# Attention and two MLPs on one core: other homes and another order for the first five pairs of heads

## The chip, the cores and the metric

The kernel runs on one core of one Trainium2 chip. The metric is the device time of one execution in microseconds. Three executions of the kernel before took 939.34, 941.24 and 942.3 us; the median is 941.24 us. The profile comes from one more execution, which took 943.38 us.

## The reference

Causal attention with a bias per position, for 4 batches of 8 heads, 576 positions and 64 elements a head, and then two MLPs over the 2304 tokens. The core of it:

```python
scores = scale * np.matmul(q, k.transpose(0, 1, 3, 2))
s_pos = np.maximum(s, 0.0)
cum = np.cumsum(s_pos, axis=-1)
bias = -(cum[:, :, :, None] - cum[:, :, None, :])
scores = np.where(causal, -1000000000.0, scores + np.minimum(bias, 0.0))
scores = scores - np.max(scores, axis=-1, keepdims=True)
attn = np.exp(scores)
attn = attn / (np.sum(attn, axis=-1, keepdims=True) + 1e-09)
attn_out = np.matmul(attn, v)
# x = attn_out as (2304, 512)
h = x @ w_in;   r = np.maximum(h, 0.0);  x = (r * r) @ w_out      # first MLP
h = x @ w2_in;  out = np.maximum(0.01 * h, h) @ w2_out            # second MLP
```

All inputs and outputs are float32. d_model is 512, d_ff is 2048.

## The kernel before, in words

The 32 heads are worked off as 16 pairs. A pair lies on the 128 partitions as two heads of 64. Its 576 query rows are cut into four kinds of work: kind 0 (query tiles 0 and 1), kind 2, kind 3 (query tiles 2 and 3) and kind 4 (the last 64 rows of both heads in one tile). `STEPS` gives seven slots a pair: two each (one per head, `e`) for kinds 0, 2 and 3, and one for kind 4. The loop over `y` in `attention` goes through the 112 slots of the 16 pairs.

For one kind the work goes through four engines. TensorE makes the scores (`scores`, L458 and L470) into a PSUM tile `S` or `h`. VectorE adds the mask, stores the sum in an SBUF tile `t` and takes the row maximum (`maxima`, L486). ScalarE takes the exponential in place and sums the row (`exponentials`, L510). TensorE transposes `t` in 64-row pieces into two PSUM banks with the tag `tr` (`flip`, L525), and ScalarE (kinds 0 and 2, L548) or VectorE (kinds 3 and 4, L546) copies them into `pT0`, `pT1` and `pX`. `values` (L567) multiplies `v` with these: region 0 is the first 256 query rows, region 1 the other 320. `gather` (L577, ScalarE) copies the product to `xo`; `inverse`, `spread` and `scale` (L583, L584, L602, L608, L612) divide it by the row sums; `store` sends it to DRAM.

What sets the order:

- The tile `t` has four buffers (`TB`), taken in turn by every slot. The tag `tr` has four banks, taken in turn by `flip`, `values` and `spread`: 12 in a pair, so that each use finds the same bank in each pair. A use waits until the reader of the bank's last content is done.
- `S` is one tile of two banks, `h` are two banks. In the first five pairs kinds 0 and 3 write `S`, kinds 2 and 4 write `h`. So the scores of kind 3 wait until both reductions of kind 0 are done, and the scores of kind 0 of the next pair wait until both of kind 3 are.
- `Y` holds a pair's turned q and k, in four quarters: `ql`, `kh`, `qh`, `kl`. In pairs 0 to 4 (`x < PLAIN`) the scores are plain float32 products, and only `kh` and `qh` are written (`turn`, L428); the quarters 0 and 3 lie unused. From pair 5 on all four are used.
- TensorE's order within a slot is written by hand (`in_order`). On VectorE and ScalarE a scheduler sets the order when the program is built.

Between these run two other streams: the weights of the first MLP are loaded and cut into two parts (`load_w`, L114, L118, L120, L122, L123, L170, L173), two chunks in five slots from slot 11 on; and from slot 36 on, after pair 4, `fill` puts products of the first MLP (L655) between the steps of attention. Pairs 0 to 4 are `ALONE`: they have no such filling on TensorE. The products of the first MLP's block 0 need the output of pairs 0 to 3.

Within pairs 0 to 4 `values` of region 0 comes in slot 6 and of region 1 in slot 10 (counted from the pair's first, so in the next pair's slot 3), and `gather` one slot later. In the slot in which region 1 of pair x is multiplied, kind 0 of pair x + 1 is transposed, behind it.

Of the kernel before, what the change touches and what calls it, by code (L numbers as in the profile page):

```python
# [8 lines left out]
F32 = mybir.dt.float32  # L9
# [14 lines left out]
def attention_then_two_mlps(  # L24
# [28 lines left out]
    P = 128  # L53
# [20 lines left out]
    AHEAD = 20  # L74
    PLAIN = 5
    ALONE = 5
    KINDS = (0, 2, 3, 4)
    STEPS = ((0, 0), (0, 1), (2, 0), (2, 1), (3, 0), (3, 1), (4, 0))

# [395 lines left out]
    def maxima(at, x, kind, e):  # L475

        p = pairs[x]
        t = at.tile([P, S], F32, tag="t", name="t", bufs=TB)
        m = at.tile([P, 16], F32, tag="m", name="m", bufs=TB + 1)

        def reduce(sc, msk, a, z, first, m):
            return nc.vector.tensor_tensor_reduce(t[:, a:z], sc, msk, -QK_SCALE, first, ALU.add, ALU.min, m).ins  # L486

        sc = p.sc[kind][e]
        if kind == 0:
            tiles = ((0, P, 0), (P, 3 * P, 1))  # L490
            for a, z, c in tiles:
                done = reduce(sc[:, a:z], mask[:, S - z + a:], a, z, 3.0e38, m[:, c:c + 1])
        elif kind == 4:
            tiles = ((0, S, 0),)
            reduce(sc[:, :S // 2], mask[:, :S // 2], 0, S // 2, 3.0e38, m[:, 1:2])
            done = reduce(p.sc[kind][1][:, :S // 2], mask4, S // 2, S, m[:, 1:2], m[:, 0:1])
        else:
            tiles = ((0, (kind + 1) * P, 0),)
            done = reduce(sc[:, :(kind + 1) * P], mask[:, S - (kind + 1) * P:], 0, (kind + 1) * P, 3.0e38, m[:, 0:1])
        if kind == 0 and e == 0:  # L500
            p.sums = at.tile([P, 16], F32, tag="sums", name="sums", bufs=4)
        T = {0: 0, 2: 2, 3: 3, 4: 4}[kind]
        p.t = t
        return t, m, tiles, p.sums, 2 * T + e, done

    def exponentials(t, m, tiles, sums, c0):
# [4 lines left out]
                                        accum_out=sums[:, s0:s0 + 1])  # L511
        return done.ins

    def flip(at, x, kind, ts):

        p = pairs[x]
        banks = [bank("tr") for _ in range(2)]
        w = 3 if kind == 0 else kind + 1
        n = 0
        for t in ts:  # L520
            for c in range(w):
                a = min(c * P, S - P)
                for r in range(2):
                    hs = slice(64 * r, 64 * r + 64)
                    nc.tensor.transpose(banks[r][:, 64 * n:64 * n + 64], t[hs, a:a + P], ident[hs, hs])  # L525
                n += 1
        if kind == 0:
            p.pT[0] = at.tile([P, 2, 3, P], F32, tag="pT0", name="pT0")
        if kind == 2:
# [20 lines left out]
    def values(x, region):  # L550
# [5 lines left out]
        for c in range(2 if region == 0 else 5):  # L556
# [4 lines left out]
                mm.append((c, a, [p.pT[1][:, e, c, a:] for e in range(2)]))  # L561
            else:
                mm.append((c, NR1 - 64, [p.pX[:, 1 - e] for e in range(2)]))
        start = len(nc.cur_bb.bb.instructions)
        for y, (c, a, rhs) in enumerate(mm):
            for e in range(2):
# [96 lines left out]
    def attention(at, mg, mx):  # L663
# [131 lines left out]
        for y in range(end + 14):  # L795
# [6 lines left out]
                behind = [args[-1], exponentials(*args[:-1])]  # L802
            fill(y, 0)
            tiled = len(nc.cur_bb.bb.instructions)
            for px in (x - 1, x):
                if not 0 <= px < len(pairs):
                    continue
                k0 = y - n * px
                for region in range(2):
                    if k0 == values_at(px, region):  # L810
                        pairs[px].po[region] = values(px, region)
            for z in (y - LAG, y - 1):
                zx, zs = divmod(z, n)
                kind, e = STEPS[zs]
                if 0 <= z < end and (e or kind == 4) and (z == y - 1) == (kind == 3 and zx >= ALONE):
                    flip(at, zx, kind, [live.pop(i) for i in range(z - e, z + 1)])
            if y + 1 < end and STEPS[(y + 1) % n][1] == 0:
                last = len(KINDS) * x + KINDS.index(STEPS[st][0])
                while asked <= last + (2 if last + 2 < AHEAD else 1):
# [4 lines left out]
            for px in (x - 1, x):  # L824
# [1 line left out]
                    continue  # L826
                k0 = y - n * px
                for region in range(2):
                    if k0 == values_at(px, region) + 1:
                        gather(at, px, region, pairs[px].po[region])  # L830
                portions = ((9, 0, 2), (13, 2, 5)) if px < ALONE else ((13, 0, 5),)
                for when, a, b in portions:
# [323 lines left out]
```

## Time and profile before

| | |
|---|---|
| median of 3 runs | 941.24 us |
| lowest, highest | 939.34, 942.3 us |
| the profiled execution | 943.38 us |
| its span, first to last instruction | 941.6 us |
| TensorE busy | 902.7 us (96%) |
| VectorE busy | 708.2 us (75%) |
| ScalarE busy | 578.6 us (61%) |
| GpSimd busy | 181.8 us (19%) |

The span lies 1.78 us under the execution's own time. The first 93 us of the span are the pairs without filling (0 to 4) and the step into pair 5; attention with filling ends at about 335 us. In the tables of stretches below, each engine has its busy microseconds and, in brackets, its number of instructions; PEclk is TensorE's granted clock, where 1.00 is 2.4 GHz and 0.50 is 1.2 GHz.

### The profile page before, as it was taken

How to read it: one execution, taken by the hardware profiler on the slowest of the kernel's cores; microseconds unless marked ns; L12 is line 12 of the kernel's file. 1: busy time of each engine (PE TensorE's matmuls, PEld its weight loads, DVE VectorE, ACT ScalarE, POOL GpSimd, SP SyncE). 2: the span in 40 equal slices, each digit the busy share in tenths (PEclk: the TensorE clock that was granted, in tenths of full speed). 3: DMA queues.
4: the chain of work that ended last, by engine and by line, in shares of the span. 5: the costliest groups of instructions: out<-in, count | busy, mean ns of one | idle time of the engine just before them, and what ended most of it. 6: DMA issues, size and time to landing. Idle time of an engine off the chain costs nothing.

```text
span 941.6 us, 16406 instructions
## 1 busy us (share of the span) xinstructions
PE 902.7 (96%) x5902; PEld 809.2 (86%) x5902; DVE 708.2 (75%) x1286; ACT 578.6 (61%) x1076; POOL 181.8 (19%) x290
## 2 busy tenths in 40 slices
PE   5877999999999999999999999999999999999997
PEld 3545777777777778989999999999999999999997
DVE  6789774877784348489797898788478788786974
ACT  5687877877796444366565555586677764344442
POOL 4357652333350001000213101001111000000000
PEclk9988999999999999999999999999999999999999
DMA  8865847896954177857749434767758585727303
GB/s 158 183 166 146 209 129 192 234 239 212 240 175 159 58 235 278 294 200 231 241 133 339 163 107 149 242 219 281 275 189 313 183 268 137 184 51 204 97 12 56
DMA packets 229569, 178.48 MB, mean 190 GB/s; under 512 B 139600, under 2 KB 206352, under 8 KB 229488
## 3 DMA queue, kind: packets, MB, share of 16 engines
q1 hardware_dynamic: 192568, 105.13, 41.5%
q10 hardware_dynamic: 27048, 38.16, 11.1%
q0 software_dynamic: 9872, 34.15, 10.5%
q8 instruction: 46, 0.75, 0.3%
q14 instruction: 35, 0.29, 0.1%
HBM read 111.25 MB, written 66.13 MB: 188 GB/s over the span
## 4 chain that ended last, share of the span: by engine, by line
PE 56%; issue 10%; DVE 6%; DMA 6%; ACT 2%; POOL 1%; ACTq 0%; SPq 0%; POOLq 0%; DVEq 0%
PE q L858 34%; PE h L655 16%; DVE op L965 3%; PE tr L567 2%; PE S L470 2%; PE tr L525 2%; DMA gp<-gscr 1%; DMA gp<-zscr 1%; DMA gp<-qscr 1%; PE S L458 1%; DVE gp L959 1%; DMA zscr<-post 1%; DMA xscr<-xo 1%; DVE wt L122 1%; POOL zscr L1027 1%
## 5 line engine op out<-in xcount | busy, mean ns | idle before, releaser
L858 PE MATMUL q<-op,w 128*128 128x384 f32 x3024 | 527.9, 335 | 6.5 <-DVE op L965 4.3
L858 PEld LDWEIGHTS q<-op,w 128*128 128x128 f32 x3024 | 523.6, 188 | 10.5 <-DVE op L965 6.6
L964 ACT ACTIVATE op<-gp 128x768 fp32r<-128x768 f32 x189 | 158.0, 845 | 152.1 <-PE q L858 125.4
L655 PE MATMUL h<-xs,w 128*128 128x512 f32 (+1 forms) x960 | 213.1, 376 | 2.3 <-DVE xs L616 1.7
L965 DVE TENSOR_TENSOR op<-gp,op 128x768 fp32r<-128x768 f32 x189 | 177.7, 952 | 40.6 <-ACT op L964 39.3
L655 PEld LDWEIGHTS h<-xs,w 128*128 128x128 f32 x960 | 164.5, 190 | 40.0 <-issue 6.0
L510 ACT ACTIVATE t<-t,m 128x128 f32<-128x128 f32 (+2 forms) x144 | 83.2, 579 | 48.6 <-DVE m L486 44.1
L486 DVE CUSTOM_DVE_ANT_0 t<-S,mask 128x128 f32<-128x128 f32 (+2 forms) x129 | 56.3, 476 | 49.2 <-PE S L470 24.0
L638 ACT ACTIVATE gs<-h 128x512 f32<-128x512 f32 (+1 forms) x80 | 43.7, 548 | 46.3 <-PE h L655 45.8
L186 POOL DMA_DIRECT2D wscr<-wt x48 | 26.7, 555 | 233.5 <-DVE wt L123 231.8
L931 DVE TENSOR_TENSOR post<-q,post 128x768 f32<-128x768 f32 (+1 forms) x55 | 51.6, 939 | 15.6 <-PE q L858 15.2
L567 PE MATMUL tr<-pT,v 128*64 128x320 f32 (+3 forms) x384 | 50.1, 405 | 5.0 <-DVE pT L546 5.0
L470 PE MATMUL S<-Y 64*128 64x128 f32 (+3 forms) x324 | 41.5, 373 | 12.8 <-DVE Y L428 7.5
L123 DVE SCALAR_TENSOR_TENSOR wt<-wst,wt 128x512 uint32<-128x512 uint32 x64 | 50.4, 787 | 3.9 <-POOL wt L122 3.2
L911 ACT ACTIVATE post<-q 128x768 f32<-128x768 f32 (+1 forms) x56 | 43.8, 782 | 12.5 <-PE q L858 12.4
L114 ACT ACTIVATE wt<-wst 128x512 f32<-128x512 f32 x64 | 42.2, 660 | 12.9 <-DMA wst<-in_moe_w_in_dram 7.9
L567 PEld LDWEIGHTS tr<-pT,v 128*64 128x64 f32 x384 | 25.9, 143 | 27.8 <-issue 7.8
L525 PEld LDWEIGHTS tr<-ident,t 64*128 64x128 f32 x800 | 31.3, 138 | 21.3 <-issue 8.0
L118 DVE TENSOR_SCALAR wt<-wt 128x512 uint32<-128x512 uint32 x64 | 32.7, 511 | 20.0 <-ACT wt L114 19.6
L891 ACT ACTIVATE post<-post 128x768 f32<-128x768 f32 x36 | 30.4, 844 | 26.0 <-DVE post L931 25.8
L525 PE MATMUL tr<-ident,t 64*128 64x64 f32 x800 | 39.6, 230 | 5.4 <-ACT xo L577 4.9
L199 DVE TENSOR_TENSOR w<-wq,w 128x512 fp32r<-128x512 f32 x49 | 33.3, 687 | 14.7 <-ACT w L198 14.7
(115 smaller groups left out, 918.6 us busy)
## 6 DMA issues: line engine op xcount, KB each, us to landing
gscr<-gs ACTq DMA_DIRECT2D x36, 512.0 KB
gp<-gscr SPq DMA_DIRECT2D x48, 384.0 KB
qscr<-post ACTq DMA_DIRECT2D x48, 384.0 KB
gp<-qscr SPq DMA_DIRECT2D x48, 384.0 KB
wscr<-wt POOLq DMA_DIRECT2D x48, 256.0 KB, 4.4
wst<-in_moe_w_in_dram SPq DMA_DIRECT2D x19, 512.0 KB
wst<-in_moe_w_out_dram SPq DMA_DIRECT2D x16, 512.0 KB
wst<-in_moe_w_out_dram POOLq DMA_DIRECT2D x16, 512.0 KB, 5.0
```

Of the source, the lines that this page charges most:

```text
L123: nc.vector.scalar_tensor_tensor(t, hw, 0xC0000000, t, ALU.bitwise_and, ALU.bitwise_or)
L470: nc.tensor.matmul(p.sc[kind][e][:, a:z], qs[hs, T * P:(T + 1) * P], ks[hs, :z - a], start=(n == 0 and y == 0), stop=(n == len(tiles) - 1 ...
L486: return nc.vector.tensor_tensor_reduce(t[:, a:z], sc, msk, -QK_SCALE, first, ALU.add, ALU.min, m).ins
L510: done = nc.scalar.activation(t[:, a:z], t[:, a:z], AF.Exp, bias=m[:, c:c + 1], scale=-1.0, accum_out=sums[:, s0:s0 + 1])
L525: nc.tensor.transpose(banks[r][:, 64 * n:64 * n + 64], t[hs, a:a + P], ident[hs, hs])
L567: p.anchor = nc.tensor.matmul(po[64 * e:64 * e + 64, a:n], p.vr[:, c, e], rhs[e], start=(y == 0), stop=(y == len(mm) - 1), skip_group_chec ...
L655: nc.tensor.matmul(h[:, :w], win[fc][:, a, c * P:(c + 1) * P], xs[j, c][:, z, :w], start=(c == 0 and y == 0), stop=(c == KC - 1 and y == 2))
L858: i = nc.tensor.matmul(*args, skip_group_check=True, **kw).ins
L911: done = nc.scalar.activation(t[:, xs], acc, AF.Copy)
L931: done = nc.vector.tensor_tensor(t[:, xs], acc, t[:, xs], ALU.add)
L964: a = nc.scalar.activation(t[:, 0], src, AF.Copy)
L965: c = nc.vector.tensor_tensor(t[:, 1], src, f32(t[:, 0]), ALU.subtract)
```

## The change

Four edits, all for pairs 0 to 4. First, kind 3's masked scores and exponentials go into the unused quarters 0 and 3 of `Y` instead of two buffers of `t`, so that only five slots in seven take a buffer of `t`. Second, in the slot in which region 1 is multiplied with v, the transposes of the next pair's kind 0 now stand ahead of that product. Third, `gather` of region 0 is written one slot earlier in the source. Fourth, TensorE multiplies the identity with itself into banks whose content nobody reads: 512 columns ahead of kind 4's transposes in pairs 0 to 4, 256 columns ahead of region 1's product in pairs 0 to 3, and three times 128 columns behind kind 4's transposes in pair 4.

```diff
+    WARM = 5
@@ maxima
-        t = at.tile([P, S], F32, tag="t", name="t", bufs=TB)
+        if kind == 3 and x < PLAIN:
+            t = f32(p.Y[:, 3 * e])
+        else:
+            t = at.tile([P, S], F32, tag="t", name="t", bufs=TB)
@@
+    def idle(to):
+
+        n = to.shape[1] // P
+        nc.tensor.matmul(to, ident, ident.unsqueeze(1).to_broadcast([P, n, P]), start=True, stop=True)
+
@@ flip
+        if kind == 4 and x < WARM:
+            idle(banks[0])
...
+        if kind == 4 and x == WARM - 1:
+            for _ in range(3):
+                idle(banks[1][:, 3 * P:])
@@ values
+        if region and x < WARM - 1:
+            idle(po[:, :2 * P])
@@ attention
-            for px in (x - 1, x):
...
-                        pairs[px].po[region] = values(px, region)
-            for z in (y - LAG, y - 1):
...
+            for early in (True, False):
+                for px in (x - 1, x):
+                    if early or not 0 <= px < len(pairs):
+                        continue
...
+                            pairs[px].po[region] = values(px, region)
+                for z in (y - LAG, y - 1):
...
+                    if early != (kind == 0 and zx < ALONE):
+                        continue
...
-                    if k0 == values_at(px, region) + 1:
+                    if k0 == values_at(px, region) + (region or px >= ALONE):
                         gather(at, px, region, pairs[px].po[region])
```

TensorE, the stretch in pair 4's time in which region 1 of pair 3 is multiplied. `tr` are the banks of transposes and products with v, `ident` the identity, `ex` the row sums' inverses, `S` the scores of kind 3. Before, from the transposes of kinds 3 and 4 (one run of 26) to those of kind 0:

```order
L525 MATMUL tr<-ident,t 128x64 x26
L470 MATMUL S<-Y 128x512 x2
L470 MATMUL S<-ag_88 128x512 x2
L602 MATMUL tr<-ident,ex 128x128 x2
L567 MATMUL tr<-pT_889,v 64x320 x6
L567 MATMUL tr<-pT_889,v 64x192 x2
L567 MATMUL tr<-pX,v 64x64 x2
L525 MATMUL tr<-ident,t 128x64 x12
```

The same stretch of the changed kernel:

```order
L536 MATMUL tr<-ident,Y 128x64 x16
L521 MATMUL tr<-ident 128x512
L536 MATMUL tr<-ident,t 128x64 x10
L471 MATMUL S<-Y 128x512 x2
L471 MATMUL S<-ag_88 128x512 x2
L618 MATMUL tr<-ident,ex 128x128 x2
L536 MATMUL tr<-ident,t 128x64 x12
L521 MATMUL tr<-ident 128x256
L583 MATMUL tr<-pT_887,v 64x320 x6
L583 MATMUL tr<-pT_887,v 64x192 x2
L583 MATMUL tr<-pX,v 64x64 x2
```

The twelve transposes of kind 0 moved ahead of the product with v, kind 3's sixteen read `Y`, and the two products of the identity stand ahead of kind 4's transposes and ahead of the product with v.

VectorE, the start of pair 2. `S` and `h` are scores, `m` the row maxima, `kr` and `qr` the raw keys and queries of pair 3, `sums` the row sums, `wt` a chunk of weights. Before, from the first transpose of pair 3's keys to the first copy of pair 1's kind 4:

```order
L428 STREAM_TRANSPOSE Y<-kr 128x576
L123 SCALAR_TENSOR_TENSOR wt<-wst,wt 128x512
L486 ISA t,m<-S,mask 128x128
L486 ISA m 128x1
L486 ISA t,m<-S,mask 128x256
L486 ISA m 128x1
L428 STREAM_TRANSPOSE Y<-qr 128x576
L546 COPY pT_456<-tr 128x8x64 x2
L486 ISA t,m<-h,mask 128x384
L486 ISA m 128x1
L546 COPY pT_456<-tr 128x4x64
```

In the changed kernel, where all four reductions of kind 0 stand directly ahead of this piece and the copies of kind 4 behind it:

```order
L119 TENSOR_SCALAR wt<-wt 128x512
L624 TENSOR_TENSOR xo<-xo,tr 128x256
L628 TENSOR_TENSOR xo<-xo,tr 64x64 x2
L490 ISA t,m<-h,mask 128x384
L490 ISA m 128x1
L599 TENSOR_SCALAR sums<-sums 128x4
L124 SCALAR_TENSOR_TENSOR wt<-wst,wt 128x512
L600 RECIPROCAL sums<-sums 128x4
L119 TENSOR_SCALAR wt<-wt 128x512
L560 COPY pT_454<-tr 128x8x64 x2
L429 STREAM_TRANSPOSE Y<-kr 128x576
L429 STREAM_TRANSPOSE Y<-qr 128x576
```

The two transposes of keys and queries moved from between the reductions of kind 0 to between the copies of kinds 3 and 4; the sums of kind 0, which need its exponentials, moved from behind the copies to ahead of them; and pair 0's last scaling of `xo` and two steps on weights came in.

ScalarE, the same place: from the end of pair 1 to the exponentials of pair 2's kind 0 (128 and 256 columns, twice). `pT` are copies of transposes, `wt` and `wst` steps on weights. Before:

```order
L548 ACTIVATE pT_456<-tr 128x2x3x64 x2
L510 ACTIVATE t,sums<-t,m 128x576
L114 ACTIVATE wt<-wst 128x512
L120 ACTIVATE wst<-wst 128x512
L577 ACTIVATE xo<-tr 128x256
L510 ACTIVATE t,sums<-t,m 128x128
L510 ACTIVATE t,sums<-t,m 128x256
L510 ACTIVATE t,sums<-t,m 128x128
```

And in the changed kernel:

```order
L514 ACTIVATE t,sums<-t,m 128x576
L562 ACTIVATE pT_454<-tr 128x2x3x64 x2
L115 ACTIVATE wt<-wst 128x512
L121 ACTIVATE wst<-wst 128x512
L514 ACTIVATE t,sums<-t,m 128x128
L514 ACTIVATE t,sums<-t,m 128x256
L514 ACTIVATE t,sums<-t,m 128x128
L593 ACTIVATE xo<-tr 128x256
L514 ACTIVATE t,sums<-t,m 128x256
```

The exponentials of kind 4 moved ahead of kind 2's copies, and the gather of region 0 into `xo` (L577, now L593) moved from ahead of kind 0's exponentials to behind three of the four.

## Rows read from the trace of the kernel before

**Rows 1.** Busy time by stretch: start:end, length, engines, clock.
```profile
93.30:335.00 241.70, 241.36 (x1918) 184.22 (x1918) 159.00 (x436) 178.78 (x426) 86.36 (x128) 1.00 0.66 185
```

**Rows 2.** The same view, from a pair's first reduction to the product of region 1.
```profile
19.57:25.64 6.07, 2.22 (x22) 1.07 (x19) 5.20 (x21) 2.92 (x11) 0.00 (x0) 0.99 0.70 142
35.00:41.01 6.01, 3.16 (x41) 1.83 (x37) 5.78 (x20) 4.65 (x15) 3.22 (x5) 1.00 0.93 167
47.94:56.38 8.44, 5.42 (x45) 2.65 (x41) 8.05 (x24) 6.72 (x22) 5.55 (x8) 0.79 0.49 134
64.92:71.86 6.94, 3.95 (x44) 2.28 (x44) 6.90 (x22) 6.94 (x20) 6.10 (x7) 1.00 1.08 237
```

**Rows 3.** The same view, the product of region 1 with v in three pairs.
```profile
25.64:29.47 3.83, 3.83 (x20) 1.94 (x21) 0.94 (x5) 0.71 (x2) 1.31 (x5) 0.56 0.87 275
41.01:43.21 2.20, 2.20 (x20) 1.34 (x21) 1.37 (x7) 0.71 (x2) 1.28 (x2) 1.00 0.83 152
56.38:60.20 3.82, 3.82 (x20) 1.91 (x20) 1.37 (x7) 1.60 (x4) 2.57 (x2) 0.57 0.47 137
```

**Rows 4.** The same view, pair 4 and the step into the filled part.
```profile
64.92:82.05 17.13, 12.40 (x138) 8.21 (x138) 16.21 (x45) 14.36 (x40) 13.62 (x17) 1.00 0.92 213
82.05:93.30 11.25, 7.82 (x36) 5.41 (x36) 10.44 (x27) 8.97 (x24) 9.03 (x9) 0.70 0.33 103
```

**Rows 5.** VectorE's and TensorE's waits, 10 to 95 us: total, times, longest.
```profile
DVE t L486 <- PE tr L525: 7.3, 4, 3.3
...
PE tr L525 <- ACT xo L577: 4.9, 4, 2.0
```

**Rows 6.** VectorE in order of time: start, duration, line, tiles, wait before.
```profile
10.32 0.29 DVE L486 CUSTOM_DVE_ANT_0 t<-S,mask 128x128 f32<-128x128 f32 x1 [2.90 <-PE S L470]
...
11.44 0.77 DVE L428 STREAM_TRANSPOSE Y<-kr 128x576 f32<-128x576 f32 x1
...
29.91 0.69 DVE L486 CUSTOM_DVE_ANT_0 t<-S,mask 128x512 f32<-128x512 f32 x1 [3.33 <-PE tr L525]
...
32.90 0.42 DVE L608 TENSOR_TENSOR xo<-xo,tr 128x256 f32<-128x256 f32 x1
33.23 0.46 DVE L612 TENSOR_TENSOR xo<-xo,tr 64x64 f32<-64x64 f32 x2
...
38.42 1.25 DVE L546 COPY pT<-tr 128x512 f32<-128x512 f32 x2
...
40.07 0.42 DVE L546 COPY pT<-tr 128x256 f32<-128x256 f32 x1
```

**Rows 7.** ScalarE in order of time, pair 1's end and pair 2's start.
```profile
32.26 0.87 ACT L548 ACTIVATE pT<-tr 128x384 f32<-128x384 f32 x2
33.08 0.78 ACT L510 ACTIVATE t<-t,m 128x576 f32<-128x576 f32 x1
...
33.85 0.66 ACT L114 ACTIVATE wt<-wst 128x512 f32<-128x512 f32 x1
...
34.98 0.36 ACT L577 ACTIVATE xo<-tr 128x256 f32<-128x256 f32 x1
35.40 0.40 ACT L510 ACTIVATE t<-t,m 128x128 f32<-128x128 f32 x1
...
35.80 0.49 ACT L510 ACTIVATE t<-t,m 128x256 f32<-128x256 f32 x1
```

**Rows 8.** TensorE in order of time, behind the product of region 1 at full clock.
```profile
43.21 0.59 PE L525 MATMUL tr<-ident,t 64*128 64x64 f32 x12
43.73 0.75 PE L458 MATMUL h<-Y,lp 128*128 128x288 f32 x2
...
45.16 0.59 PE L525 MATMUL tr<-ident,t 64*128 64x64 f32 x12
```

**Rows 9.** The page's groups: line, operation, count, busy us, mean ns, idle before.
```profile
L123 DVE SCALAR_TENSOR_TENSOR wt<-wst,wt 128x512 uint32<-128x512 uint32 x64 | 50.4, 787 | 3.9 <-POOL wt L122 3.2
...
L118 DVE TENSOR_SCALAR wt<-wt 128x512 uint32<-128x512 uint32 x64 | 32.7, 511 | 20.0 <-ACT wt L114 19.6
```

More of the change, by code (lines that the diff above doesn't have):

```diff
@@ L804, in attention @@
             tiled = len(nc.cur_bb.bb.instructions)
-            for px in (x - 1, x):
[L806 to L810, printed above, removed]
-                        pairs[px].po[region] = values(px, region)
-            for z in (y - LAG, y - 1):
[L813 to L816, printed above, removed]
+            for early in (True, False):
+                for px in (x - 1, x):
+                    if early or not 0 <= px < len(pairs):
+                        continue
+                    k0 = y - n * px
+                    for region in range(2):
+                        if k0 == values_at(px, region):
+                            pairs[px].po[region] = values(px, region)
+                for z in (y - LAG, y - 1):
+                    zx, zs = divmod(z, n)
+                    kind, e = STEPS[zs]
+                    if early != (kind == 0 and zx < ALONE):
+                        continue
+                    if 0 <= z < end and (e or kind == 4) and (z == y - 1) == (kind == 3 and zx >= ALONE):
+                        flip(at, zx, kind, [live.pop(i) for i in range(z - e, z + 1)])
             if y + 1 < end and STEPS[(y + 1) % n][1] == 0:
```

## The prediction, on record before the result was known

> **What bounds the kernel now.** I read the busy time by stretch first, then the two stretches' waits, then the engines in order of time. From 93.3 us to the end of attention TensorE is busy 241.36 of 241.70 us at full clock [rows 1], and the order of its work from there on is the same before and after. So whatever brings TensorE to that point earlier is carried to the end, and whatever happens ahead of it on another engine counts only through that. The question is when the stream begins that is full at 93.3 us.
>
> Ahead of it no engine is full, and the work runs in a ring: VectorE reduces the scores, ScalarE takes exponentials, TensorE transposes, VectorE copies, TensorE multiplies with v. I cut each pair at two marks: A, its first reduction on VectorE, and E, the start of the product of region 1 for the pair ahead of it, which begins when VectorE's copies are done. The A marks are 19.57, 35.00, 47.94, 64.92 and 82.05, the E marks 25.64, 41.01, 56.38 and 71.86 [rows 2, 4]. From A to E VectorE is busy nearly throughout (5.78 of 6.01 and 6.90 of 6.94 us in pairs 2 and 4). From E to the next A it is not.
>
> Two things make E to A long. The product of region 1 takes 2.20 us at a granted clock of 1.00, but 3.83 and 3.82 us in the two pairs where the clock stood at 0.56 and 0.57, mostly its lower level of 1.2 GHz [rows 3]: 1.62 us more. Before the first fall TensorE had been busy 2.22 of 6.07 us, before the product that kept its clock 3.16 of 6.01 [rows 2]. And VectorE stands still until the transposes of kind 0 behind that product are done, since kind 3's reductions need a buffer of t: 7.3 us in four waits, 3.33 us in the longest [rows 5, 6].
>
> **The change part by part.** *Kind 3 in Y.* The wait of 3.33 us goes: kind 3's reductions need no buffer of t and run beside the product. What is late next is kind 4's first reduction, which needs the scores that TensorE makes behind the product.
>
> *Transposes ahead of the product.* TensorE's sum is unchanged: 0.52 us (43.21 to 43.73, [rows 8]) move from behind 2.20 us to ahead of them. They use the bank that VectorE's copies of kind 4 release half way, so nearly all of it lies under the second half of these copies. I cost it at nothing; without that cover it is 0.5 us a pair.
>
> *Identity products.* Full-height float32 products of 512 columns are not in the trace. Kind 4's scores are the nearest: two halves of 288 columns, each in float32 and once more with the bias, take 1.43 us (43.73 to 45.16, [rows 8]), so one half 0.72 us; by columns, 512 cost at most 1.27 us, and half of that if the bias takes as long as the rest. I take 0.8 us, and 0.4 us for 256 columns. The Trainium skill ("FP8 and Floating Point Precision", section "TensorE Precision Notes") counts four passes through the array for true float32, which by my estimate makes 512 columns 0.85 us at 2.4 GHz; the sum would be the same within 0.1 us a pair. The 512 columns stand in front of transposes that waited 4.9 us in four places for the gather [rows 5], so they are hidden. The 256 columns write the bank that the last copy ahead of the product releases: they come after the wait, and cost 0.4 us on the path in pairs 0 to 3.
>
> *The gather one slot earlier.* The schedule does not follow the source: on ScalarE the gather of region 0 now stands behind three of the next pair's four exponentials of kind 0, not ahead of them. I cost it at nothing, since kind 4's transposes behind it are needed later than before.
>
> *The order on VectorE.* This is the part with a price. The sums of kind 0 now stand ahead of the copies. They wait for four exponentials of 0.40 and 0.49 us [rows 7] and hold the copies, both transposes of the next pair's keys and queries (0.77 us, [rows 6]) and kind 4's copies behind them. VectorE works strictly in order: it stood idle 3.33 us ahead of one reduction while later work was ready [rows 6]. The Trainium skill says the same ("TensorE: Matmul & The Clock Gate", section "Architectural detail: the array is 16× 32×32, not 1× 128×128": ACT and DVE are strict FIFO); if VectorE could pass its waiting sums, the sum below would be 2.5 us better, 936.2 us.
>
> *The sum, pair by pair.* Pair 0: kind 4's exponential no longer stands behind two copies of 0.82 us (32.26 to 33.08, [rows 7]); its maximum comes 0.2 us later than the copies would have begun, so A1 is 0.6 us earlier, 18.95.
>
> Pair 1, A to E: four reductions 1.12 us (10.32 to 11.44, [rows 6]); the exponentials end at 2.3; sums and reciprocal 0.25; one reduction and kind 3's copies 1.65 (38.42 to 40.07, [rows 6]); keys and queries 1.5; kind 4's copies 0.94 (40.07 to 41.01, [rows 2, 6]): 6.65 us, E1 25.6, as before. E to A: 0.4 + 2.20 + 0.72 until kind 4's first scores, its reductions end at 4.8, its exponential takes 0.97 with the read-out, the sums 0.25: 6.1 us. A2 is 31.7, before 35.00.
>
> Pair 2, A to E: 1.12; a step L118 0.51 [rows 9]; pair 0's last scaling 0.8 (32.90 to 33.69, [rows 6]); one reduction 0.47; then VectorE waits 1.0 us, because ScalarE still has two copies of 0.82, L114 and L120 of 1.13 (33.85 to 34.98), four exponentials and a gather of 0.42 [rows 7]; sums 0.25; L123 and L118 0.79 and 0.51 [rows 9]; kind 3's copies 1.2; 1.5; 0.94: 9.1 us against 6.01 [rows 2]. E2 is 40.8, before 41.01. E to A: VectorE now needs 3.5 us until kind 4's reductions, TensorE 3.3; 1.1 for these, 0.97, 0.25, and 0.6 for ScalarE's weights in front: 6.4 us. A3 is 47.2, before 47.94.
>
> Pair 3: the same terms with the wait for ScalarE at 1.8 us and one step L123 less ahead of the copies: 9.6 us, E3 56.8 (before 56.38), and 6.6 us to A4 at 63.4 (before 64.92).
>
> Pair 4 and the step into the stream: VectorE is busy 16.21 of 17.13 and 10.44 of 11.25 us [rows 4], with the same work after. Only its idle 1.7 us can go. The last pieces of the first MLP's input stand ahead of the weights now, where two steps on weights stood before: I take 1.0 us of it. The stream begins 1.5 + 1.0 = 2.5 us earlier. The profiled execution would take 943.38 - 2.5 = 940.9 us; the three runs' median lies 2.14 us under that execution, so the forecast is 938.7 us.
>
> Unknown terms: the clock in each of three pairs (1.62 us for the product and 0.4 for the identity products at half speed, 2.0 in all); the waits for the sums (none to twice the 2.8 us); the 1.0 us of the last step (0 to 1.7). All good: 938.7 - 2.8 - 0.7 = 935.2, and near 933 if pair 3's A to E, 8.44 us before, also shrinks to pair 2's 6.01 [rows 2]. All bad is the third rival.
>
> **The rivals.** *The clock falls all the same.* Kind 3's scores now come early, and TensorE then has nothing for 2.7 to 2.9 us until VectorE's copies are done in pairs 2 and 3. For it: waits of at most 2.0 us for the gather were the longest that TensorE had, and the clock fell all the same [rows 3, 5]. Against it: with the identity products TensorE is busy about 3.4 us between kind 3's transposes and E, more than the 3.16 us of the pair that kept its clock. One fall gives 2.0 us of the 2.5 back: 940.7 us.
>
> *Hidden anyway.* VectorE, ScalarE and GpSimd are at 95, 84 and 80% in pair 4 [rows 4]. If the weights pace pairs 4 and 5, what was gained ahead is waited for there: 941 us. For it: the weights' steps are the same in number. Against it: beside the product VectorE is busy only 0.94 of 3.83 and 1.37 of 2.20 us [rows 3], room that such steps can use.
>
> *VectorE's sums stop the ring, and the product is slow in every pair.* Its place is A to E of pairs 2, 3 and 4: the longer this is, the longer TensorE's gap, so that the product runs at the lower level in all three. The price is 3 x 2.0 = 6.1 us against the 2.5 gained: 943.38 + 3.6 = 947.0 for the profiled execution, 944.8 us for the median. It decides from the point where two of the three products take 3.8 us. For it: A to E grows from 6.01 to 9.1 us by my own sum. Against it: as under the first rival.
>
> *The edits do nothing.* The order shows that all four stand in the program except the gather, so this is left out.
>
> **How the numbers follow.** A measurement of this kernel can tell 0.3%, 2.8 us, from no change. My case has a chance of 0.50, and 2.5 us lie at that bound: with the good ends 0.40 of it is faster, 0.10 the same. The clock's single fall 0.20: 0.17 the same, 0.03 faster. Hidden anyway 0.13, the same. The stopped ring 0.17, slower. Together faster 0.43, same 0.40, slower 0.17. The range is 933 to 944 us: it takes in the good ends and the first two rivals and leaves out the stopped ring and some of the very good ends. The likeliest case alone goes from 935 to 940.
>
> **What would show it.** Right: region 1's product at 2.2 us in pairs 1 to 3; no wait of VectorE's kind 3 reductions for transposes; A marks near 31.7, 47.2, 63.4; a new wait of VectorE's sums for ScalarE of 1 to 2 us a pair; the stream 2.5 us earlier and nothing gained or lost behind 93 us. Wrong: products of 3.8 us; waits of the first MLP's products for the weights behind 90 us; or a VectorE that does not stop at its sums.

## The result, and the profile after

The changed kernel takes 955.48 us (median of 5 runs, 953.57 to 956.23), the kernel before 942.30 us in the same comparison: a ratio of 1.0142, 95% interval 1.0122 to 1.0162. That is slower by some 13 us and outside the range forecast. The profiled execution took 956.23 us and spans 954.4 us, 12.8 more than before.

First the stream at the end of the work, busy time by stretch (start:end, length, busy time of PE, PEld, DVE, ACT and POOL, granted clock, DMA):

```profile
67.32:89.75 22.43, 18.07 (x153) 10.69 (x149) 19.00 (x50) 15.27 (x38) 14.97 (x20) 0.77 0.73 156
89.75:102.34 12.59, 6.87 (x27) 4.03 (x26) 11.13 (x26) 9.26 (x24) 9.13 (x10) 0.86 0.33 103
106.28:345.00 238.72, 238.39 (x1893) 182.24 (x1894) 157.29 (x434) 176.02 (x421) 81.10 (x122) 1.00 0.64 182
```

As in [rows 1], TensorE is full once the stream runs. But the stream starts at 102.34 us, not at 93.3, and its first product is slow too. Attention's last product starts at 333.30 us, before at 322.54: 10.8 of the 12.8 us lie ahead of it. (Its last step, a scaling on VectorE, ends at 329.4 us in before, so the 335 us given at the start for the end of attention are some 6 us late.) The rest of the span, 621.1 us after and 619.1 before, lies between 615.3 and 621.1 in the profiled executions of all twenty kernels of this study; after's is the longest, I see no relation to the edits, and what sets it stays open. Pair 4 takes 22.43 us where [rows 4] have 17.13, and the step behind it 12.59 for 11.25.

The same view from each pair's first reduction (A) to the identity product of 256 columns, which starts when VectorE's copies are done; it answers to [rows 2]:

```profile
18.98:25.68 6.70, 4.78 (x53) 2.74 (x49) 5.58 (x22) 3.19 (x13) 0.00 (x0) 1.00 0.75 146
31.88:40.27 8.39, 6.23 (x63) 3.52 (x63) 7.55 (x28) 5.83 (x18) 5.53 (x9) 1.00 0.87 147
48.44:57.94 9.50, 6.16 (x62) 3.47 (x58) 8.35 (x28) 6.24 (x18) 5.36 (x8) 1.00 0.43 119
67.32:77.88 10.56, 6.20 (x52) 3.11 (x48) 10.46 (x30) 7.78 (x20) 8.28 (x11) 0.70 1.05 189
```

And the product of region 1 in pairs 1 to 4 and in the step behind them, for [rows 3]:

```profile
26.31:28.58 2.27, 2.27 (x22) 1.41 (x21) 1.23 (x5) 2.27 (x8) 1.31 (x5) 1.00 0.90 268
40.90:44.83 3.93, 3.93 (x22) 2.05 (x21) 1.83 (x6) 2.19 (x6) 1.27 (x1) 0.57 0.99 276
59.09:62.47 3.38, 3.38 (x22) 1.84 (x21) 1.41 (x4) 3.24 (x9) 0.86 (x1) 0.66 0.35 102
79.03:82.68 3.65, 3.65 (x22) 1.93 (x21) 1.29 (x5) 1.91 (x6) 1.42 (x2) 0.61 0.22 77
102.34:106.28 3.94, 3.94 (x23) 2.06 (x24) 0.00 (x0) 0.61 (x2) 1.55 (x2) 0.57 0.37 123
```

Four of five products run mostly at the clock's lower level of 1.2 GHz, though TensorE was busy for longer ahead of them than before (6.23 of 8.39 us in pair 2, 3.16 of 6.01 in [rows 2]). The waits of 10 to 102 us (total, times, longest) tell what took the place of the one in [rows 5]; two lines are VectorE's, two TensorE's, and the second fence has TensorE's wait for the copies before:

```profile
DVE t L490 <- PE h L459: 8.1, 4, 3.2
DVE sums L599 <- ACT t L514: 5.4, 5, 1.5
...
PE tr L536 <- DVE pX L560: 8.1, 4, 2.6
...
PE tr L521 <- DVE xo L628: 1.9, 1, 1.9
```

```profile
PE tr L567 <- DVE pT L546: 5.0, 4, 1.4
```

VectorE's wait of 7.3 us for the transposes (`tr`) is gone but for 0.2 us, as forecast. Its place is taken by 8.1 us for kind 4's scores, which stand behind the products (1.89 us behind the fast one of pair 1, up to 3.2 behind the others), and TensorE now waits 8.1 us in four places for VectorE's copies, where it had waited 5.0. VectorE in order of time, pair 4, shows what these copies stand behind:

```profile
70.69 0.39 DVE L119 TENSOR_SCALAR wt<-wt 128x512 uint32<-128x512 uint32 x1
71.10 0.56 DVE L490 CUSTOM_DVE_ANT_0 t<-h,mask 128x384 f32<-128x384 f32 x1
...
71.59 1.28 DVE L560 COPY pT<-tr 128x512 f32<-128x512 f32 x2
72.79 1.13 DVE L599 TENSOR_SCALAR sums<-sums 128x4 f32<-128x4 f32 x1
73.83 2.00 DVE L632 TENSOR_TENSOR xs<-xh,xs 128x512 fp32r<-128x512 f32 x1
75.75 0.72 DVE L124 SCALAR_TENSOR_TENSOR wt<-wst,wt 128x512 uint32<-128x512 uint32 x1
76.39 0.41 DVE L560 COPY pT<-tr 128x256 f32<-128x256 f32 x1
...
83.53 0.46 DVE L490 CUSTOM_DVE_ANT_0 t<-h,mask 128x288 f32<-128x288 f32 x1 [3.21 <-PE h L459]
```

The copies of kind 4 are the one at 76.39 and those behind it. They stand behind a piece of the first MLP's input (`xs`) and a step on weights, 2.72 us; later VectorE stands still for 3.21 us until the slow product lets the scores through. TensorE there:

```profile
71.06 0.52 PE L536 MATMUL tr<-ident,t 64*128 64x64 f32 x10
...
74.24 0.37 PE L536 MATMUL tr<-ident,t 64*128 64x64 f32 x1
77.08 0.87 PE L536 MATMUL tr<-ident,t 64*128 64x64 f32 x11 [2.48 <-DVE pX L560]
77.88 1.22 PE L521 MATMUL tr<-ident 128*128 128x256 f32 x2
79.03 3.53 PE L583 MATMUL tr<-pT,v 128*64 128x320 f32 x16
```

The transposes that these copies read are the ten at 71.06 us: their data were ready 4.8 us before they were copied. The eleven at 77.08 and the identity product wait for the copies, and the product comes behind both.

### The profile page after: what moved, and what is told of

Same layout as the page of the kernel before. It is cut to its first block, busy times and chain, and to the rows that moved or that the text cites. A ratio compares the mean times of both kernels' runs of the same rounds, so it can differ in the third digit from the quotient of the medians.

```text
span 954.4 us, 16437 instructions
## 1 busy us (share of the span) xinstructions
PE 915.1 (96%) x5926; PEld 813.6 (85%) x5926; DVE 710.9 (74%) x1286; ACT 578.8 (61%) x1076; POOL 181.6 (19%) x290
## 4 chain that ended last, share of the span: by engine, by line
PE 62%; issue 8%; DVE 4%; DMA 4%; ACT 2%; POOL 1%; POOLq 0%; DVEq 0%; ACTq 0%; SPq 0%
PE q L877 40%; PE h L671 16%; PE tr L583 2%; PE S L471 2%; DVE op L984 2%; PE tr L536 2%; DMA gp<-zscr 1%; PE S L459 1%; DMA gp<-qscr 1%; DVE gp L978 1%; DMA xscr<-xo 1%; DMA wst<-in_moe_w_out_dram 0%; PE tr L618 0%; DMA xh<-xscr 0%; DVE gp L976 0%
## 5 line engine op out<-in xcount | busy, mean ns | idle before, releaser
L877 PEld LDWEIGHTS q<-op,w 128*128 128x128 f32 x3024 | 523.6, 188 | 12.8 <-DVE op L984 8.2
L514 ACT ACTIVATE t<-t,m 128x256 f32<-128x256 f32 (+4 forms) x134 | 76.0, 568 | 51.6 <-DVE m L490 50.7
L490 DVE CUSTOM_DVE_ANT_0 t<-S,mask 128x128 f32<-128x128 f32 (+4 forms) x119 | 49.4, 459 | 50.5 <-PE S L471 30.9
L536 PEld LDWEIGHTS tr<-ident,t 64*128 64x128 f32 x720 | 28.4, 140 | 28.7 <-issue 19.4
L583 PE MATMUL tr<-pT,v 128*64 128x320 f32 (+3 forms) x384 | 52.2, 420 | 0.0
L910 ACT ACTIVATE post<-post 128x768 f32<-128x768 f32 x36 | 30.4, 844 | 25.6 <-DVE post L950 25.5
L536 PE MATMUL tr<-ident,t 64*128 64x64 f32 x720 | 37.2, 232 | 8.9 <-DVE pX L560 8.1
```

What stands on the lines that cost most here:

```text
L514: done = nc.scalar.activation(t[:, a:z], t[:, a:z], AF.Exp, bias=m[:, c:c + 1], scale=-1.0, accum_out=sums[:, s0:s0 + 1])
L583: p.anchor = nc.tensor.matmul(po[64 * e:64 * e + 64, a:n], p.vr[:, c, e], rhs[e], start=(y == 0), stop=(y == len(mm) - 1), skip_group_chec ...
L877: i = nc.tensor.matmul(*args, skip_group_check=True, **kw).ins
```

## The experiments

All eighteen at once; every ratio is to the runs of before on the same chip. "Products" are the times of region 1's product in pairs 1 to 4 and in the step behind them (2.3 is full clock, 4.3 the lower level throughout), A4 the start of pair 4, S that of the step's product, with which the stream begins. The last three columns are read from one profiled execution of each kernel, the time and the ratio from all its runs.

| kernel | us | ratio to before, interval | products, us | A4 | S |
|---|---|---|---|---|---|
| before (first three runs) | 941.24 | 1 | 3.9 2.3 3.9 2.3 2.3 | 64.92 | 93.29 |
| after | 955.48 | 1.0142 (1.0122, 1.0162) | 2.3 3.9 3.4 3.7 3.9 | 67.32 | 102.34 |
| e1_split | 951.44 | 1.0096 (1.0069, 1.0123) | 3.1 3.9 2.3 3.8 4.1 | 66.71 | 101.62 |
| e2_onlyY | 948.02 | 1.0061 (1.0039, 1.0082) | 2.3 4.3 4.3 2.3 4.2 | 65.89 | 99.74 |
| e3_noY | 947.33 | 1.0077 (1.0051, 1.0104) | 4.0 2.3 3.6 3.0 2.3 | 66.05 | 99.16 |
| e4_noidle | 943.74 | 1.0024 (1.0004, 1.0044) | 2.3 3.5 2.3 2.3 2.3 | 61.35 | 91.95 |
| f1_idle_in_noidles_order | 945.06 | 1.0043 (1.0022, 1.0064) | 2.3 3.7 2.3 3.0 2.3 | 63.37 | 95.25 |
| f2_noidle_in_afters_order | 948.18 | 1.0073 (1.0055, 1.0091) | 2.3 3.7 4.3 4.0 2.4 | 66.05 | 100.16 |
| f3_before_with_idle | 941.00 | 1.0004 (0.9978, 1.0030) | 4.0 2.3 2.3 2.3 2.3 | 63.44 | 94.26 |
| f4_split_noidle | 941.86 | 1.0011 (0.9994, 1.0029) | 2.3 2.3 3.6 4.3 2.3 | 61.65 | 92.75 |
| g2_after_steps_behind_copies | 949.71 | 1.0088 (1.0061, 1.0115) | 2.3 3.8 3.8 2.3 2.3 | 66.85 | 98.97 |
| g3_split_idle_fixed_order | 946.09 | 1.0051 (1.0025, 1.0077) | 4.3 2.3 4.0 2.3 2.6 | 66.23 | 99.81 |
| g4_split_noidle_weights_early | 948.01 | 1.0076 (1.0049, 1.0103) | 2.3 3.1 2.3 2.3 3.1 | 64.03 | 96.10 |
| g5_before_weights_early | 947.41 | 1.0061 (1.0041, 1.0081) | 2.3 2.3 3.4 4.3 2.5 | 67.09 | 98.51 |
| h1_after_no_256 | 950.60 | 1.0084 (1.0051, 1.0117) | 2.3 2.3 4.3 4.3 3.3 | 67.14 | 101.08 |
| h2_early_alone | 944.93 | 1.0030 (1.0007, 1.0054) | 2.3 2.3 2.8 4.3 3.2 | 60.94 | 93.59 |
| h3_before_weights_late | 941.05 | 0.9997 (0.9982, 1.0011) | 4.0 2.3 2.3 2.3 2.3 | 62.70 | 93.42 |
| h4_split_noidle_weights_late | 940.07 | 0.9978 (0.9957, 0.9999) | 4.3 3.9 2.3 3.5 2.3 | 65.37 | 92.65 |
| i1_both_fixed | 950.90 | 1.0071 (1.0043, 1.0098) | 2.3 4.0 3.5 2.3 3.4 | 67.67 | 100.38 |
| i2_split_noidle_weights_later | 949.43 | 1.0057 (1.0033, 1.0080) | 3.4 2.3 3.5 2.3 3.5 | 68.31 | 98.82 |

The executions of one kernel differ, and its clock with them. g3's twelve lie between 942.1 and 952.0 us, and the profiled one, at 951.56, is among the longest; h2's profiled one took 940.87 us, its median is 944.93. In e1 the two executions of 947.6 and 947.8 us have a granted clock of 0.993 over the span, the four of 951 to 954 us one of 0.987 to 0.989. So a slow product in the table is a reading of one execution, and no run shows that the same product is slow in the next.

**Which edit.** Four kernels take one part away or leave one alone. e1 gives kind 3's t tiles of its own:

```diff
-            p.Y = at.tile([P, 4, S], F32R, tag="Y", name="Y", bufs=YB)
...
+            p.kh, p.qh = [at.tile([P, S], F32R, tag=z, name=z, bufs=YB) for z in ("kh", "qh")]
...
-            t = f32(p.Y[:, 3 * e])
+            t = f32(at.tile([P, S], F32R, tag=("ql", "kl")[e], name="t3", bufs=YB))
```

> As after, but kind 3's t no longer shares a buffer with the keys and queries: the unused quarters are tiles of their own (same memory), so that the transposes of the next pair's keys and queries on VectorE need not wait for kind 3's transposes on TensorE. In the order on VectorE they move back from between the copies to the reductions of kind 0; the sums stay ahead of the copies. Theory 'shared buffer': these 1.5 us between the copies lengthen A to E of pairs 2 to 4 and TensorE's gap ahead of the product; without them A to E of pairs 2 and 3 is 1.5 us shorter, at least two of the three products of 3.3 to 3.9 us come back to 2.2 us, and the time is 940 to 946 us. Theory 'waiting sums': the sums alone stop the ring; they are where they were, so products stay slow and the time is 951 to 956 us.

e2 keeps this edit alone, e3 takes it back, e4 takes the calls of `idle` out:

```diff
-        if kind == 4 and x < WARM:
-            idle(banks[0])
...
-        if region and x < WARM - 1:
-            idle(po[:, :2 * P])
```

> Only the first edit: kind 3's exponentials in Y; transposes, gather and identity products as before the change. The order on VectorE is nearly that of after. Theory 'shared buffer' (and 'waiting sums' too, since both come with this edit): slow by itself, 950 to 956 us, with keys and queries between the copies. Theory 'identity products or transposes in front cost the time': near or under before, 938 to 944 us.

> The other three edits without the first: t of kind 3 in a buffer of its own kind again, transposes of kind 0 ahead of the product, identity products, gather a slot earlier. Theories 'shared buffer' and 'waiting sums': the wait of VectorE for the transposes shrinks by about a product's time, the clock is helped, 936 to 942 us. Theory 'identity products or transposes in front': 946 to 953 us.

> After without the three kinds of identity product. If they stand in the path, as the traces of after have them (256 columns take 0.7 to 1.15 us behind the wait for VectorE's copies in pairs 0 to 3, with the clock falling all the same): 3 us faster, 951 to 953 us. If they keep the clock for anything that counts: the product of pair 1, 2.2 us in after, is at 3.8 and the time is 957 us or more. If they are hidden: 954 to 956 us.

e1 moved the keys and queries as meant, yet its products stayed slow in four of five places: 951.4 us, in the range of 'waiting sums', so 'shared buffer' failed. e3 lies in the range of 'identity products or transposes in front', e2 and e4 in none of theirs. e2 and e3 are both slower than before, though they share no edit. e4 is the surprise: without the identity products one of the five products is slow, not four, and nearly all of the loss is gone. But it is still 1.0024 times before, for all that pair 4 begins 3.6 us earlier. One reason may stand in ScalarE's order of time in e4:

```profile
75.66 0.66 ACT L121 ACTIVATE wst<-wst 128x512 uint32<-128x512 uint32 x1 [3.35 <-DMA wst<-in_moe_w_in_dram]
```

A step on weights waits 3.35 us for its DMA with the exponentials and the gather queued behind it: rival "hidden anyway". Another stands behind S. e4's stream begins 1.3 us before that of before, but its last product of attention starts 2.0 us later (324.52 and 322.54), because TensorE has two more waits and a lower clock just behind S; first e4's stretch, then the same of before:

```profile
100.00:105.00 5.00, 4.18 (x17) 3.65 (x17) 3.91 (x8) 3.68 (x9) 3.48 (x4) 0.67 0.55 168
```

```profile
100.00:105.00 5.00, 5.00 (x42) 4.16 (x43) 4.41 (x12) 4.15 (x11) 3.23 (x4) 1.00 0.68 190
```

**The products or the order they bring.** Each edit reorders VectorE and ScalarE, as I take it because the scheduler places steps by the time it expects TensorE to take. f1 to f3 separate the two: a table of numbers chains the first 360 instructions of VectorE and 320 of ScalarE in the order that another kernel has.

```diff
+        for name, order in ORDERS.items():
+            engine = getattr(nc, name).engine
+            mine = [i for i in nc.cur_bb.bb.instructions if i.engine == engine and ...]
+            for a, b in zip(order, order[1:]):
+                tc.add_manual_dep(mine[b], mine[a].name, ..., reason="in_order")
```

> After with all its identity products, but the first 360 instructions of VectorE and 320 of ScalarE are chained in the order that e4_noidle has without them. Theory 'order': the identity products cost little themselves; the time estimates that the scheduler holds for them move steps of the weights ahead of VectorE's copies, and that costs: within 3 us of e4_noidle, 943 to 947 us, the products of pairs 2 and 3 as there (3.8 and 2.2 us). Theory 'the products themselves' (0.7 to 1.2 us of 256 columns behind each wait, 1.1 us of 512 ahead of the transposes): 949 to 956 us.

> The other way round: no identity product, VectorE and ScalarE chained in the order that after has. Theory 'order': slow without any identity product, 950 to 956 us, with weights' steps of 1.1 us between the transposes of keys and queries and kind 4's copies in pair 3 and the products of pairs 2 to 4 at 3.3 to 3.9 us. Theory 'the products themselves': 942 to 946 us as e4_noidle.

> The kernel before with the identity products alone, VectorE and ScalarE chained in the order of before, so that nothing but TensorE's work differs. If the products hold the clock and are hidden: the products of pairs 1 and 3 come from 3.83 to 2.2 us, 2 x 1.6 us less, minus four times 0.4 to 0.7 us for the 256 columns behind the wait: 937 to 941 us. If they hold no clock and stand in the path: four times 0.7 to 1.2 us and up to 1.1 us each for the 512 columns: 943 to 948 us.

Both theories hold in part. After's order without one identity product is slow by itself (f2, 1.0073, though its 948.18 us lie between its two ranges), f1 lies in the range of 'order', f3 at the slow end of its first, and the same products cost 0.0069 in after's order, but 0.0019 in e4's and 0.0004 in before's, neither of which the intervals tell from nothing. f1's identity products stand at the same place in TensorE's order as after's. So what they cost depends on the order around them. f3 has the 256 columns elsewhere in time; TensorE in pair 3:

```profile
54.63 0.70 PE L524 MATMUL tr<-ident 128*128 128x256 f32 x2
56.51 2.16 PE L586 MATMUL tr<-pT,v 128*64 128x320 f32 x16 [1.18 <-DVE pT L563]
```

There the 256 columns run ahead of the wait, 1.9 us before the product starts, and the product keeps its clock (2.27 us, in before 3.89). In after they start behind the wait, at 77.88 in the rows above. What stands between is the second edit: the transposes moved in front wait for VectorE's copies and hold the identity product too. But this place does not decide whether a product is slow. f3's pair 1 has the 256 columns ahead of the wait too, and its product takes 3.96 us:

```profile
24.39 0.70 PE L524 MATMUL tr<-ident 128*128 128x256 f32 x2
25.74 3.85 PE L586 MATMUL tr<-pT,v 128*64 128x320 f32 x16 [0.65 <-DVE pT L563]
```

After's pair 1 has them behind the wait and a product of 2.27 us; and h3, with no identity product, has the same five times as f3 in the table. Counted over pairs 1 to 4 of the table, 15 of 24 products are slow with the 256 columns behind the wait, 25 of 52 without them, 1 of 4 in f3. What the runs do show is the granted clock over the whole span, taken over all executions: 0.9956 in f3 and 0.9907 in before on the same chip, 0.9937 in f1 and 0.9893 in e4 (on another chip, where before has 0.9912). In these two orders the identity products, taken together, go with a higher clock, and still no time is gained; in after's order (0.9866, and 0.9857 in f2) hardly so.

f3's pair 4 begins 1.5 us earlier than that of before, its stream 1.0 us later (94.26 and 93.29), and ScalarE's rows, first f3's and then before's, show the same step on weights let go at nearly the same time:

```profile
74.56 0.66 ACT L121 ACTIVATE wt<-wst 128x512 f32<-128x512 f32 x1 [3.86 <-DMA wst<-in_moe_w_in_dram]
```

```profile
74.95 0.68 ACT L114 ACTIVATE wt<-wst 128x512 f32<-128x512 f32 x1 [2.77 <-DMA wst<-in_moe_w_in_dram]
```

**The four steps and the 256 columns.** g2 keeps after's order but for four instructions of VectorE, h1 leaves out the 256 columns, i1 does both:

```diff
 pair 3:  sums, copies of kind 3, keys, queries,
-         L124 wt, L119 wt, copies of kind 4
+         copies of kind 4, L124 wt, L119 wt
 pair 4:  copies of kind 3, sums,
-         L632 xs, L124 wt, copies of kind 4
+         copies of kind 4, L632 xs, L124 wt
```

> After, all four edits and all identity products, VectorE and ScalarE chained in after's own order, with four instructions of VectorE moved: in pair 3 the two steps on weights (0.65 and 0.46 us), in pair 4 the piece of the first MLP's input (2.00 us) and the step on weights (0.72 us), from just ahead of kind 4's copies to just behind them. Theory 'these steps hold the copies, TensorE's gap grows and the clock falls': A to E is 1.1 us shorter in pair 3 and 2.7 in pair 4, and if the clock holds for one of the two products 1.3 to 1.6 more: 948 to 952 us against 955.5. Theory 'the four steps only change places with other waits (the weights, the products)': 953 to 956 us.

> After without the identity products of 256 columns in front of the product with v in pairs 0 to 3, VectorE and ScalarE chained in after's order; those of 512 and of 128 columns stay. Theory 'the 256 columns cost, since they start behind the wait': 0.4 to 1.15 us each on the way and a later product, most of the 7.3 us: 949 to 951.5 us. Theory 'the 512 columns cost, since they stand ahead of transposes that are ready': 953 to 956 us.

> After with four steps of VectorE moved behind kind 4's copies in pairs 3 and 4 as in g2, and without the identity products of 256 columns as in h1; the rest of VectorE's and ScalarE's order is after's. If the two costs add: 955.5 - 5.8 - 4.9 = 944.8, so 943.5 to 946.5 us. If they are one cost: 948.5 to 951 us.

All three came out in a range: g2 in that of "these steps hold the copies", h1 in that of "the 256 columns cost", i1 in that of "one cost". Each brings back 0.005 to 0.006 of the 0.0142, both together 0.007: they don't add. The marks explain g2 better than h1. Attention's last product starts 5.1 us earlier than in after in g2, but 2.0 us in h1 (331.35 and 333.30); the other 4.0 of the 6.0 us between h1's profiled execution and after's lie behind attention, where no edit was made. In i1 the copies of pair 4 end 7.5 us behind A4 (after: 10.1), and its product has the full clock again; but VectorE then waits for ScalarE's weights, ahead of kind 4's second reduction:

```profile
79.16 0.44 DVE L496 CUSTOM_DVE_ANT_0 t<-h,mask 128x288 f32<-128x288 f32 x1
...
82.19 0.50 DVE L125 TENSOR_SCALAR wt<-wt 128x512 uint32<-128x512 uint32 x1 [2.58 <-ACT wt L121]
82.61 0.51 DVE L496 CUSTOM_DVE_ANT_0 t<-h,mask,m 128x288 f32<-128x288 f32 x1
```

**The other edits and a better version.** f4 takes e1 and e4 together, g3 puts the identity products into f4's order, h2 is the second edit alone; g4, h4 and i2 move f4's steps on weights by -2, +2 and +4 slots (`CV` from 11 to 9, 13, 15), g5 and h3 those of before by -2 and +2.

> After without the identity products and with kind 3's t in tiles of its own in place of Y's quarters: both suspected costs away, the wait for kind 3's buffer away too. Theory 'shared buffer': keys and queries stand with the reductions of kind 0, A to E is 1.5 us shorter than in e4_noidle, whose pair 2 product ran at the lower level: 938 to 941 us, under before if the clock holds in pairs 1 to 4. If the shared buffer costs nothing: 942 to 946 us as e4_noidle.

> f4_split_noidle with the identity products put back and VectorE and ScalarE chained in that kernel's order. In f4 the products of pairs 3 and 4 ran at the lower level (4.1 us). Theory 'in a good order the products hold the clock and hide': both products at 2.2 us, minus 0.4 to 0.7 us a pair behind the wait; stream no earlier where the weights pace pair 4: 939 to 942 us. Theory 'each costs its time behind the wait': 943 to 946 us.

> Before with the second edit alone: the transposes of kind 0 in front of the products with v, in the order that the scheduler gives. If the move itself is good, VectorE's wait for these transposes (7.3 us in four places) shrinks by the product's time: 936 to 940 us. If what it frees is given back in pair 4: 940 to 943 us. If its order is bad as that of the kernel without kind 3 in Y (947.3 us): 944 to 948 us.

> f4_split_noidle with the steps on the weights (their DMAs too) two slots earlier in the source. Theory 'the weights pace pair 4': ScalarE's wait for their DMA in pair 4 (2.35 us in f4 at 75.87 us, 2.77 in before) goes, the stream starts 1.5 to 3 us earlier: 937 to 940 us. Theory 'VectorE paces pair 4': no change, 941 to 943 us, or slower by what the steps displace in pairs 1 and 2.

> The kernel before with the steps on the weights two slots earlier, as a control for g4. Theory 'the weights pace pair 4': faster than before by 1 to 3 us, 937.5 to 940 us. Theory 'the ring of pairs 1 to 4 paces': 940 to 943 us.

> Before with the steps on the weights two slots later. Two slots earlier made it 6 us slower. Theory 'steps on weights in VectorE's and ScalarE's queues hold pairs 1 to 4': fewer of them there, 1 to 4 us faster, 937 to 940 us, unless the first MLP's products then wait for weights behind 95 us. Theory 'any shift of the order costs, and the order before is a good one by luck': 943 to 947 us.

> f4_split_noidle with the steps on the weights two slots later, with the same two theories: 937 to 940 us, or 943 to 947 us.

> f4_split_noidle with the steps on the weights four slots later (h4 had two: 940.1 us). If VectorE's and ScalarE's steps on weights hold the pairs: 937 to 940 us. If the first MLP's products now wait for weights behind 92 us: 941 to 946 us.

f4 takes as long as before, just outside both of its ranges; in g3 the products cost 0.004 again, which puts it just beyond its slower range. h2 is slower than before by itself, as its third range had it. Weights two slots earlier made both kernels slower by 0.006, which speaks against "the weights pace pair 4": in g5 ScalarE's wait for their DMA from 60 to 95 us falls from 3.1 us to 0.9, and the time grows all the same, beyond both of its ranges. Two slots later is neutral for before, which fits neither theory of h3, four for f4 are worse than either range of i2, and h4 is the fastest of all, at the edge of its better range: 940.07 us, ratio 0.9978, its interval up to 0.9999. As the best of eighteen this is no gain that a measurement can tell, so no version beats before.

## Why the prediction was wrong

By its own marks, measured behind forecast: A1 18.95 and 18.98; E1 25.6 and 25.68; A2 31.7 and 31.88; E2 40.8 and 40.27; A3 47.2 and 48.44; E3 56.8 and 57.94; A4 63.4 and 67.32; start of the stream 90.8 and 102.34. A to E of pairs 2 and 3, forecast at 9.1 and 9.6 us, took 8.39 and 9.50. So the working of the order on VectorE was near, waits for the sums included (0.78 and 1.02 us in these two pairs, forecast 1.0 and 1.8), and the step on kind 3 in Y was right. In pair 3 the agreement is partly luck: its own terms add up to 9.1 us, not 9.6, and where the wait was 0.8 us shorter, two steps on weights (0.65 and 0.46 us) stood ahead of kind 4's copies that the sum doesn't have there.

**The step that failed first is the clock.** The case assumed 2.2 us in pairs 1 to 3, because "with the identity products TensorE is busy about 3.4 us between kind 3's transposes and E". In pair 2 TensorE was busy for 3.9 us between these marks (34.24 to 40.27), and for 6.2 of 8.4 us from A to E, and the clock fell all the same as the product began: the busy time that I compared is not what decides here. After's other executions have the low clock too: 0.985 to 0.988 over the span in all five, where before has 0.99 on average in 114. Each slow product made the next A later. A3 was 1.2 us late and A4 3.9, so 2.7 us came in pair 3: 1.2 from its product, 0.75 from the identity product ahead of it, and part of the rest from VectorE, where a step on weights directly ahead of A4 waited and took long, though TensorE had finished the scores at 65.36:

```profile
65.54 1.75 DVE L124 SCALAR_TENSOR_TENSOR wt<-wst,wt 128x512 uint32<-128x512 uint32 x1 [0.97 <-POOL wt L123]
```

**The price of the 256 columns** was taken at 0.4 us. Behind the wait they took 0.63 us at full clock (25.68 to 26.31, 40.27 to 40.90) and 1.15 at the lower level (57.94 to 59.09, 77.88 to 79.03): 3.6 us in four pairs for 1.6. The 512 columns, taken at 0.8 us and estimated at 0.85 from four passes, took 1.06 (19.70 to 20.76); the bound that the prediction had worked out by columns, 1.27 us for 512 and so 0.64 for 256, was the better figure. I knew that the 256 columns come after the wait. Whether this also kept them from holding the clock is not shown.

**The largest error is the step "pair 4 and the step into the stream".** I had 27.4 us from A4 to the stream, "with the same work after", and let it only gain. It took 35.0, 6.6 more than before: 5.3 in pair 4, and 1.3 in the step behind it, where the first MLP's products wait 3.1 us for VectorE's `xs` (before 1.4). I did not look where the new order puts this work: two steps of 2.72 us ahead of kind 4's copies, a gap of 2.48 us on TensorE in consequence, and for VectorE 19.00 us busy in the pair where it had 16.21 and 3.4 us idle where it had 0.9. f2 shows that the order does most of this without any identity product (34.1 us from A4), and g2 that moving four instructions takes 2.9 us off it, 1.4 of them because the product of pair 4 ran at full clock there. The slow first product of the stream adds 1.7 us.

**The rivals.** The third, the stopped ring, was the right one in its sign and its trigger (the products of pairs 2, 3 and 4 all slow); I gave it 0.17 and a price of 6.1 us, since it too let pair 4 be neutral. Its mechanism was only part of the truth: e4 has its sums ahead of the copies too and keeps the clock in four of five products; it is the whole order around the copies (f2, g2) and, in that order, the identity products (h1) that cost. "Hidden anyway" may have its piece: in e4 and f3 ScalarE waits 4.1 and 3.9 us for the weights from 60 to 95 us, in before 3.1. But g5 shortens this wait and is slower, so what it takes back is not shown.

**What stays open.** In nine of the twenty kernels A4 is at most 65.4 us and the stream begins at 92.0 to 96.1; in the other eleven A4 is at least 65.9 and it begins at 98.5 to 102.3. A pair 4 that begins a little later ends much later. These are single executions, and since those of one kernel differ by up to some 10 us (g3), a kernel may have both kinds. From 60 to 95 us ScalarE waits 2.2 to 3.3 us in after, h1 and e1 for VectorE's step on weights and not at all for the weights' DMA, in e4 4.1 us for the DMA; but i2 and g5 are late with neither wait long. Why this is so steep I could not settle.

## What to carry to other kernels

A higher clock need not pay: unread products went with a higher granted clock in f1 and f3, and no time was gained. Look for what such a product waits for itself, and for edits that move it behind the wait, where its own time counts. Don't read one slow product of one execution as a property of the kernel. In a kernel that a scheduler orders, measure an edit once in the old order, by chaining the engines, and once in its own; here the same products cost nothing that can be told in one order and 0.7% in another. And where a change reorders the work, price every stretch from its own new order, the last one too: "the same work" is not the same time.

## What the runs showed of the hardware

**The clock can fall late.** In after's pair 2 TensorE is empty from 38.18 to 39.78 us at a granted clock of 1.00, works at 0.99 for 1.12 us, and gets 0.57 in the product behind. h1, with the same order and the same 1.60 us empty, keeps 1.00. The first fence is after's, the second h1's:

```profile
38.18:39.78 1.60, 0.00 (x0) 0.03 (x1) 1.60 (x5) 0.00 (x0) 1.54 (x3) 1.00 0.73 132
39.78:40.90 1.12, 1.12 (x14) 0.72 (x14) 1.12 (x5) 0.49 (x2) 0.40 (x1) 0.99 0.90 221
```

```profile
37.35:38.96 1.61, 0.01 (x2) 0.03 (x2) 1.61 (x5) 0.00 (x0) 1.55 (x3) 1.00 0.81 152
38.96:41.72 2.76, 2.76 (x32) 1.84 (x32) 2.76 (x10) 2.14 (x6) 0.47 (x2) 1.00 0.97 198
```

In these two executions a gap of one length thus stands ahead of a product that is 1.7 us longer in one and not in the other; that the gap makes the clock fall is not shown by itself. In the table a fall that is gone in one pair often stands in another (f4, g3, i1). I take this for the same thing, but no run shows it, and it could as well be the execution that differs and not the kernel.

**VectorE beside GpSimd.** The same operation on `xs` took 2.00 us at 73.83 us, while GpSimd ran from 72.46 to 75.29, and 0.67 at 89.05, where GpSimd was idle; after's rows, first GpSimd's, then VectorE's:

```profile
72.46 2.83 POOL L434 TENSOR_TENSOR Y<-yt,Y 128x576 fp32r<-128x576 f32 x2
```

```profile
89.05 0.67 DVE L632 TENSOR_TENSOR xs<-xh,xs 128x512 fp32r<-128x512 f32 x1
```

The Trainium skill ("SBUF — State Buffer", section "SBUF: two separate sides") says that VectorE with two inputs in SBUF and a GpSimd instruction that reads SBUF lock each other out of a shared pair of ports; these rows agree, by 1.3 us. Such a step is cheap beside a product and dear ahead of a copy that TensorE waits for.
